# The block mask's room and place, two turns and six weight sums in another order (RWKV-6 attention, then a two-layer SiLU block)

## Chip, cores and metric

One core of one Trainium2 chip. The metric is device time in microseconds, from the launch to the end of the slowest (here the only) core. Before the change: 570.13 us, median of 3 runs (570.03 to 570.25). Engines are named as in the profile: PE (matrix products), PEld (its weight loads), DVE (VectorE), ACT (ScalarE), POOL (GpSimd), SP (the engine that issues most DMAs).

## The reference

Inputs r, k, v, w are (4 batches, 8 heads, 768 tokens, 48) in float32. First the recurrence of RWKV-6, then a bridge, then a two-layer block with SiLU:

```python
for t in range(S):
    cur = einsum('bhd,bhe->bhde', u[None] * k[:, :, t], v[:, :, t])
    y[:, :, t] = einsum('bhd,bhde->bhe', r[:, :, t], state + cur)
    state = w[:, :, t, :, None] * state + einsum('bhd,bhe->bhde', k[:, :, t], v[:, :, t])
x = y.transpose(0, 2, 1, 3).reshape(3072, 384)
h = x @ w_in                       # 384 x 2048
out = (h / (1 + exp(-h))) @ w_out  # 2048 x 384
```

## The kernel before

**Units.** The 768 tokens are cut into 6 chunks of 128, and the 4 batches into 2 pairs: 12 units, numbered 0 to 11 ("the fourth unit" is number 3). A unit goes through the attention of its chunk, and its 256 rows of x then go through the two layers. The attention is made level by level: at level l (0 to 6) blocks of 2^l tokens are joined, keys (tile tk) and queries (tile tr) are multiplied by products of w (tiles tw), PE forms scores, and a mask says which scores are kept (keep_masked, L715). The diagonal, the "bonus" with u, is added apart: own_mask (L334) in units 0 to 3, and from unit 4 on a bonus by blocks of 8 tokens, which needs another mask, the block mask (make_block_mask, L480; read by block_write, L565).

**Masks.** There is one int8 mask of 128 x 2 x 64 for each level 1 to 6 (L332). Those of levels 5 and 6 are read for units 0 and 1 alone; later units copy those scores with ACT (keep_level, L792, its L800). The block mask has a room of its own in the tile spare (L464), and is made in unit 3, in the group of mix that also holds prepare of level 5 (L995): one iota on POOL (L484), then two small operations and two masks on DVE (L486, L487, L489).

**Turns.** From unit 2 on, a unit's w, k and r are turned by DVE (turn, L347; its L361 is a transpose of 128 x 512, two for each name). After a turn of w POOL forms the products (product, L404; L410), after one of k ACT and POOL make the keys (odd_ones, L656; start_keys, L666; grow_own, L651; grow_keys, L642). Unit 3's turns stand in the first three groups of mix(3) (L987, L988).

**Update of the state.** update (L901) lets PE form the new part, ACT scales the old state (L927), and DVE adds the two (L932).

**Weights.** w_in and w_out come in 16 pieces. Each is rounded into a pair of parts by ACT (L228, L230, L236) and DVE (L247, L248) and put together by POOL (add_weight, L256; L260). Pieces 0 to 7 are w_in, 8 to 15 w_out. Two rooms of temps are shared by all pieces in turn, so ACT's L230 for a piece waits until POOL has added the piece two before it.

**The layers.** Units 0 to 2 have a plain first layer (up, L1073; L1078), unit 0 a plain second one (down, L1262; L1267). From unit 1 on the second layer is made by seven products in place of eight (quarter, L1304; L1329), for which DVE forms sums of gt (sums, L1287; L1300: four each time) and four sums of w_out (weight_sums, L1283; L1285, numbered 0 to 3 by "which"). From unit 3 on the first layer is also made of fewer products, twenty (first_part, L1194; L1185) in the order of ORDER (L1189). For these, sums of w_in are needed: weight_plan (L1099) names them, in_weight_sum (L1120; L1124) makes them on POOL or DVE. Name, operands and room of those that the change moves:

```python
"m": (e["m"], a[1, 2], a[2, 2], sub)
"q14": (e["q14"], a[1, 2], a[3, 2], add)
"u1": (a[2, 2], a[4, 1], a[3, 1], sub), "u": (a[2, 2], e["m1"], a[2, 2], add),
"q19": (a[2, 3], a[2, 3], a[2, 2], sub)
```

u and q19 are the left sides of products 11 and 19 of the first layer.

**What sets the order.** Nothing is scheduled: each engine runs its instructions in the order of the program, and waits for the others through semaphores. The order is written out by hand: lists of steps in do(...) for units 0 to 2 (L1378 to L1434), and for units 3 to 11 the groups that mix(i) returns (L961), with the steps of the layers put between the groups by their counts (L1436 to L1451). The steps of sums are added to groups at L1440 to L1446. The last list ahead of unit 3 is:

```python
do((sums, 1, 3), (y_state, 2), *both(y_values, 2), *both(update, 2), (move_x, 2), *blocks[5:])
```

A tile of a pool with bufs=1 that is taken again waits for the readers of the one before; ruk (L431) is such a tile, first taken in unit 3.

Of the kernel before, what the change touches and what calls it, by code (L numbers as in the profile page):

```python
# [8 lines left out]
F32 = mybir.dt.float32  # L9
BF16 = mybir.dt.bfloat16  # L10
I8 = mybir.dt.int8
# [27 lines left out]
def kernel(  # L39
# [11 lines left out]
    nc = tc.nc  # L51

    B, H, S, D = r.shape
    DM, DF = moe_w_in.shape
    L = 128
    NL = 7
    NB = 2
# [13 lines left out]
    BLK = 1 << FIRST  # L71


    const = ctx.enter_context(tc.tile_pool(name="const", bufs=1))
    pin = ctx.enter_context(tc.tile_pool(name="pin", bufs=1))
    pt = ctx.enter_context(tc.tile_pool(name="pt", bufs=2))
# [112 lines left out]
    spare = const.tile([128, NSPARE * 2 * TU], F32, name="spare")  # L189
# [132 lines left out]

    masks = {}
    first = {}
    for l in range(NL):
        c, ni = 1 << l, L >> (l + 1)

        first[l] = score[:, 0, 0].rearrange("p q t -> p (q t)")[:, l * 64:(l + 1) * 64].rearrange("p (i c) -> p i c", c=c)
        nc.gpsimd.iota(first[l], pattern=[[2 * c, ni], [0, c]], base=0, channel_multiplier=0,
                       allow_small_or_imprecise_dtypes=True)  # L330
        if l > 0:
            masks[l] = const.tile([128, NB, ni, c], I8, name=f"mask{l}")  # L332
    nc.gpsimd.memset(spread, 0.0)
    own_mask = const.tile([128, NB, L // 2, 2], I8, name="own_mask")  # L334
    for b in range(NB):
# [81 lines left out]
    ruk = {}  # L417
# [40 lines left out]
    room_b = spare[:, 0:768]  # L458
    at = 768
# [1 line left out]
    nc.gpsimd.memset(block_sums, 0.0)  # L461
    block_both = spare[:, at:at + NB * H * BLK].rearrange("p (b h s) -> p b h s", b=NB, h=H)
    at += NB * H * BLK
    block_mask = spare[:, at:at + NB * L // 4].bitcast(I8).rearrange("p (b i s) -> p b i s", b=NB, s=BLK)  # L464
    at += NB * L // 4
    assert at <= NSPARE * 2 * TU

    def at_rk(start, *dims):
# [10 lines left out]

    def make_block_mask():  # L480

        ids = spare[:, 0:2 * NB].rearrange("p (x b) -> p x b", x=2)
        index = room_b[:, 2 * NB:2 * NB + L].rearrange("p (i s) -> p i s", s=BLK)
        nc.gpsimd.iota(index, pattern=[[BLK, L // BLK], [0, BLK]], base=0, channel_multiplier=0,  # L484
                       allow_small_or_imprecise_dtypes=True)
        nc.vector.tensor_single_scalar(out=ids[:, 0].bitcast(I32), in_=tok_all, scalar=-BLK, op=ALU.bitwise_and)  # L486
        nc.vector.tensor_copy(out=ids[:, 1], in_=ids[:, 0].bitcast(I32))  # L487
        for b in range(NB):
            nc.vector.tensor_single_scalar(out=block_mask[:, b], in_=index, scalar=ids[:, 1, b:b + 1], op=ALU.is_equal)  # L489
# [465 lines left out]
    def both(fn, i, *args):  # L955
        return [(fn, i, b, *args) for b in range(NB)]
# [4 lines left out]
    def mix(i):  # L961
# [3 lines left out]
        def at(now, *steps):  # L965
            return steps if now else ()
# [17 lines left out]
               [*at(i < len(units) - NB, (turn_apart, i), (turn_k, i)), (y_state, i), *both(y_values, i), *at(ahead, *turns(i + 1)), *at(ahead and i > NFAST, *sum_steps(i + 1, 0, 1)),  # L984
                *at(i <= NFAST, (sums, i - 1, FH // 2 - 2)), *both(update, i), *at(not ahead, (move_x, i))]]
        if i < NPAIR:
            groups = [[*both(turn, i, "w"), (product, i, 0)],  # L987
                      [*both(turn, i, "k"), (odd_ones, i)], [*both(turn, i, "r"), (start_levels, i), (prepare_keys, i, 1)],  # L988
                      [(prepare, i, 1), *[(product, i, l) for l in range(1, NL)]],
                      [(burst, i, 1), (keep_level, i, 1)],  # L990
                      [(keep_level, i, 2), (go_on, i, 2)],
                      [(prepare, i, 3), (reverse_v, i), (bonus, i, 0), (bonus_sum, i, 0)],
                      [(bonus, i, 1), (burst, i, 3), (keep_level, i, 3), (bonus, i, 2)],
                      [(keep_level, i, 4), (go_on, i, 4), (bonus_sum, i, 1), (load_rk, i + 1), (load_u,)],
                      [(prepare, i, 5), (make_block_mask,)],  # L995
                      [(burst, i, 5), (keep_level, i, 5, 0), (keep_level, i, 6, 0), (go_on, i, 6), *at(i == NPAIR - 1, *both(turn, i + 1, "w")), (bonus_spread, i), (bonus_write, i, (0,)), (keep_level, i, 5, 1), (keep_level, i, 6, 1), (bonus_write, i, (1,))], *end]
            groups = list(zip(groups, (1, 1, 0, 2, 1, 1, 1, 1, 1, 2, 2, 1, 1)))
        else:
# [172 lines left out]
    def keep_banks():  # L1171

        for x in range(2):
            kept[f"h{x}"] = ps.tile([128, 512], F32, name="p_h", bufs=2)
            kept[f"o{x}"] = second[0].tile([128, 512], F32, name="p_o", bufs=2)
# [169 lines left out]
    def ups(i):  # L1345

        if i >= NFAST:
            made = [[(first_part, i, n)] for n in ORDER]
            if i == len(units) - 1:
                made[10].append((sums_of_x, i, 7))  # L1350
            made[17].append((sums, i, 0))
            made[-1].append((sums, i, 1, range(4) if i > NFAST else (0, 2)))
            return made
        steps = [[(up, i, m)] for m in range(FC // 2)]
        for m in range(FH // 2 - (1 if i == len(units) - 1 else 2)):

            steps[FH // 2 + 1 + m].append((sums, i, m))
        steps[-1].append((sums, i, FH // 2 - 1))
        return steps

    def downs(i):
        return [[(quarter, i, x)] for x in range(7)]

    def do(*steps):
        for fn, *args in steps:
            fn(*args)
# [39 lines left out]
    for m in range(1, 4):  # L1406
# [1 line left out]
    do((head_weight, 8), (join_weight, 7), (scores, 1, 5), (grow_keys, 1, 6), (add_weight,), (tail_weight, 8), (up, 0, 6),  # L1408
       (bonus_write, 1))

    do((scores, 1, NL - 1), (bonus, 2, 0), (bonus, 2, 1), (join_weight, 8), (add_weight,), (bonus_sum, 2, 0), (bonus, 2, 2), (in_weight_sum, nc.gpsimd, "m", "q14"), (up, 0, 7), (turn_apart, 1), *both(x_products, 1),
       (turn_k, 1), *both(x_copy, 1), (tail_weight, 9), (head_weight, 9),
       (join_weight, 9), (add_weight,), (in_weight_sum, nc.gpsimd, "q3", "q"), *both(update, 1), (up, 1, 0), (tail_weight, 10), (head_weight, 10), (bonus_sum, 2, 1), *both(turn, 2, "w"))
    blocks = block_loads(3)
# [6 lines left out]
    for m in range(6):  # L1421
# [5 lines left out]
    do(*blocks[0:2], (level, 2, 2), (prepare, 2, 3), (down, 0, 1, 0), (down, 0, 0, 3), (down, 0, 1, 1), (sums, 1, 0), (weight_sums, 0))  # L1427
    do(blocks[2], (burst, 2, 3), (keep_level, 2, 3), (keep_level, 2, 4), (go_on, 2, 4), (prepare, 2, 5), (reverse_v, 2), (down, 0, 1, 2),
       (bonus_spread, 2), (sums, 1, 1), *blocks[3:5], (down, 0, 1, 3))
    do((burst, 2, 5), (keep_level, 2, 5), (keep_level, 2, 6), (go_on, 2, 6), (bonus_write, 2), (up, 1, 6), (weight_sums, 1),  # L1430
       (load_values, 3), (turn_apart, 2), (turn_k, 2), (up, 1, 7), (weight_sums, 2), (sums, 1, 2))
    do((sums, 1, 3), (y_state, 2), *both(y_values, 2), *both(update, 2),
       (move_x, 2),
       *blocks[5:])  # L1434

    for i in range(3, len(units)):  # L1436
        steps = downs(i - 2) + ups(i - 1)
        groups = mix(i)
        if i == NTOK + 1:
            groups[4][0].append((weight_sums, 3))  # L1440
            for place, engine, names in ((7, nc.vector, ("n",)), (8, nc.vector, ("m1", "m2",)), (9, nc.vector, ("q12a", "q12",)), (9, nc.gpsimd, ("n13", "t",)), (11, nc.gpsimd, ("u1", "u", "q19",)),):
                groups[place][0].append((in_weight_sum, engine, *names))
        if i == NFAST + 1:
            keep_banks()
            for place, engine, names in ((5, nc.gpsimd, ("q7",)), (8, nc.gpsimd, ("q8", "q1",)), (9, nc.gpsimd, ("q5", "q9",)), (14, nc.gpsimd, ("q6", "q17",)),):
                groups[place][0].append((in_weight_sum, engine, *names))  # L1446
        for group, count in groups:
            do(*group)
            for step in steps[:count]:
                do(*step)  # L1450
            steps = steps[count:]  # L1451
# [34 lines left out]
```

## Time and profile before

| | |
|---|---|
| median of 3 timed runs | 570.13 us |
| the profiled execution | 571.49 us |
| its span, first to last instruction | 569.7 us |
| PE, PEld busy | 555.2, 516.5 us |
| DVE, ACT, POOL busy | 476.4, 274.6, 394.5 us |
| granted PE clock | 1.0 |
| PE's waits from 60 to 260 us / later | 4.6 us / none shown |

The span leaves 1.79 us of the profiled execution outside it. Busy time of an engine that is waiting for another does not count, so the share of PE (97%) says how little time PE has in which it does nothing. The unit of 42 us that repeats from 240 us on is PE's work alone. Unit 2 ends, by PE's matmuls of y, at 122 us, unit 3 at 167, unit 4 at 215.

In the views, a group of instructions is told as start, duration, engine, line, operation, output and inputs, count, and in brackets the idle time of that engine just before it and what ended it. The chain that ended last shows start, duration and what.

### The profile page before, as it was taken

The page shows a single profiled execution, that of the slowest core. Times are in us where ns is not written, and L with a number is a line of the kernel's source. Part 1 is how long each engine was busy: PE and PEld are TensorE (multiplying, and loading weights), DVE is VectorE, ACT ScalarE, POOL GpSimd, SP SyncE. Part 2 cuts the span into 40 slices and gives each one's busy share as a digit, 9 for nine tenths or more (in the row PEclk, how much of TensorE's full clock was granted, in tenths as well). Part 3 has the DMA queues.
Part 4 walks back from the last instruction along what each step waited for, and adds up shares of the span by engine and source line. Part 5 has one row for each costly group of instructions (what it writes and reads, how often), then busy time and mean ns, then how long its engine had stood idle before and what let it go on. Part 6 is the DMA issues. An engine that isn't in the chain of part 4 may idle for free.

```text
span 569.7 us, 18886 instructions
## 1 busy us (share of the span) xinstructions
PE 555.2 (97%) x7782; PEld 516.5 (91%) x7782; DVE 476.4 (84%) x744; ACT 274.6 (48%) x620; POOL 394.5 (69%) x447
## 2 busy tenths in 40 slices
PE   8989999999998999999999999999999999999997
PEld 7767776699888999899999999999999999999997
DVE  7979787988999889899989989989989989882250
ACT  5679686262371364274274274274274272371330
POOL 6998698709896998887796696696696696700000
PEclk9999999999999999999999999999999999999999
DMA  9856976445345355274465465465465462102000
GB/s 221 275 104 191 238 220 131 49 68 118 89 78 100 70 109 96 56 134 90 80 128 94 84 116 94 90 111 92 94 104 95 90 110 65 38 5 56 29 9 21
DMA packets 206485, 57.59 MB, mean 101 GB/s; under 512 B 186048, under 2 KB 198208, under 8 KB 206400
## 3 DMA queue, kind: packets, MB, share of 16 engines
q1 hardware_dynamic: 203712, 54.23, 46.2%
q10 hardware_dynamic: 2688, 2.16, 1.5%
q8 instruction: 61, 1.00, 0.8%
q14 instruction: 24, 0.20, 0.1%
HBM read 47.14 MB, written 9.18 MB: 99 GB/s over the span
## 4 chain that ended last, share of the span: by engine, by line
PE 70%; DVE 11%; POOL 8%; DMA 3%; ACT 3%; SPq 2%; issue 2%; DVEq 0%; POOLq 0%; ACTq 0%
PE p_o L1329 24%; PE p_o L1185 14%; PE p_h L1185 9%; PE p_h L1329 4%; PE p_m L1267 3%; PE p_h L1078 2%; PE p_sc L700 2%; PE p_m L864 2%; POOL tk L642 2%; DVE temps L1300 2%; PE p_sc L1329 2%; DVE score L718 2%; DMA raw<-in_k_dram 2%; PE p_m L843 1%; PE p_m L700 1%
## 5 line engine op out<-in xcount | busy, mean ns | idle before, releaser
L642 POOL TENSOR_TENSOR tk<-tk,tw 128x256 f32<-128x256 f32 x112 | 90.7, 830 | 7.5 <-DVE tw L410 3.2
L1329 PE MATMUL p_o<-own,temps 128*128 128x192 f32 x496 | 82.9, 326 | 1.6 <-DVE temps L1300 1.6
L1329 PEld LDWEIGHTS p_o<-own,temps 128*128 128x128 f32 x496 | 80.8, 190 | 2.0 <-DVE temps L1300 1.9
L1185 PE MATMUL p_o<-xt,w_in_sb 128*64 128x128 f32 x1152 | 72.3, 273 | 0.3 <-POOL w_in_sb L1124 0.3
L410 POOL TENSOR_TENSOR tw<-tw 128x256 f32<-128x256 f32 (+6 forms) x71 | 40.0, 563 | 44.8 <-DVE tw L361 41.3
L1078 PE MATMUL p_h<-xt,w_in_sb 128*128 128x256 f32 x288 | 66.1, 384 | 1.7 <-POOL w_in_sb L260 1.5
L1185 PEld LDWEIGHTS p_o<-xt,w_in_sb 128*64 128x64 f32 x1152 | 64.7, 137 | 0.7 <-POOL w_in_sb L1124 0.6
L1078 PEld LDWEIGHTS p_h<-xt,w_in_sb 128*128 128x128 f32 x288 | 53.6, 190 | 10.0 <-POOL w_in_sb L260 2.4
L493 POOL TENSOR_TENSOR ruk<-tokens_rk 128x384 f32<-128x384 f32 x48 | 53.7, 1138 | 3.9 <-DVE block_sums L530 2.0
L1329 PE MATMUL p_o<-w_out_sb,gt 128*128 128x192 f32 x308 | 54.5, 330 | 1.2 <-DVE ob L1337 1.2
L1329 PEld LDWEIGHTS p_o<-w_out_sb,gt 128*128 128x128 f32 x308 | 50.0, 190 | 2.2 <-DVE ob L1337 1.5
L624 DVE TENSOR_TENSOR tr<-tr,tw 128x512 f32<-128x512 f32 x57 | 49.7, 873 | 0.6
L651 POOL TENSOR_TENSOR tk<-tk,tw 128x256 f32<-128x256 f32 x32 | 24.8, 804 | 30.7 <-DVE tk L361 30.7
L1300 DVE TENSOR_TENSOR temps<-gt 128x512 f32<-128x512 f32 (+1 forms) x48 | 45.9, 992 | 0.0
L1334 ACT COPY partial<-p_o 128x192 f32<-128x192 f32 x31 | 9.8, 320 | 68.0 <-PE p_o L1329 61.2
L1209 ACT ACTIVATE gt<-p_o 128x512 f32<-128x512 f32 x45 | 26.0, 601 | 25.5 <-PE p_o L1185 25.4
L612 ACT COPY tk<-tk 128x256 f32<-128x256 f32 x52 | 20.9, 402 | 35.5 <-POOL tk L642 27.1
L718 DVE COPY_PREDICATED score<-mask,p_sc 128x512 f32<-128x512 int8 x42 | 31.2, 799 | 2.1 <-PE p_sc L700 1.9
L1329 PE MATMUL p_o<-w_out_sb,temps 128*128 128x192 f32 x176 | 30.4, 326 | 0.0
L1329 PE MATMUL p_h<-w_out_sb,gt 128*128 128x192 f32 x168 | 29.1, 326 | 0.0
L493 POOL TENSOR_TENSOR spare<-tokens_rk 128x384 f32<-128x384 f32 x24 | 28.5, 1199 | 0.6
L1329 PEld LDWEIGHTS p_o<-w_out_sb,temps 128*128 128x128 f32 x176 | 28.9, 190 | 0.0
(248 smaller groups left out, 1310.5 us busy)
## 6 DMA issues: line engine op xcount, KB each, us to landing
w_out_sb<-in_moe_w_in_dram SPq DMA_DIRECT2D x6, 768.0 KB, 7.8
turned<-yt SPq DMA_DIRECT2D x18, 192.0 KB, 2.7
xt<-turned SPq DMA_DIRECT2D x9, 384.0 KB, 3.3
w_out_sb<-in_moe_w_out_dram SPq DMA_DIRECT2D x4, 768.0 KB, 5.4
own<-in_moe_w_out_dram SPq DMA_DIRECT2D x4, 768.0 KB, 5.8
tokens_w<-in_w_dram SPq DMA_DIRECT2D x8, 384.0 KB, 4.4
tokens_rk<-in_r_dram SPq DMA_DIRECT2D x7, 384.0 KB, 4.4
tokens_rk<-in_k_dram SPq DMA_DIRECT2D x7, 384.0 KB, 5.5
```

Of the source, the lines that this page charges most:

```text
L410: engine.tensor_tensor(out=up, in0=t[:, :, 0::2], in1=t[:, :, 1::2], op=ALU.mult)
L493: mul = lambda out, one, two: nc.gpsimd.tensor_tensor(out=out, in0=one, in1=two, op=ALU.mult)
L612: nc.scalar.copy(out=keys(i, X[(l + 1) % 2] * L + c, [4 * c, blocks], [c, 2], [1, c]), in_=keys(i, NP * L + c, [4 * c, blocks], [NP * L + ...
L624: nc.vector.tensor_tensor(out=odd, in0=odd, in1=tw[i][l][:, :, 0::2][:, :, :, None].to_broadcast([128, Q, L >> (l + 1), c]), op=ALU.mult)
L642: nc.gpsimd.tensor_tensor(out=out, in0=have, in1=odd_products(i, l, b, *blocks), op=ALU.mult)
L651: nc.gpsimd.tensor_tensor(out=have, in0=have, in1=odd_products(i, l, b, [2, NP * ni]), op=ALU.mult)
L718: nc.vector.copy_predicated(out=dst, mask=masks[l][:, :, None].to_broadcast([128, NB, NP, ni, c]), data=sc[e].rearrange("p (b q) (i c) -> ...
L1078: nc.tensor.matmul(p_h[:, a, :], lhsT=w_in_sb[:, c, f * 128:(f + 1) * 128], rhs=xt[i][:, c, :], start=(a == 0 and c == 0), stop=(a == 1 an ...
L1185: nc.tensor.matmul(p[h:h + PD, q, :], lhsT=left[:, f:f + PD], rhs=right, start=first and q == 0, stop=q == 3, skip_group_check=True)
L1209: nc.scalar.activation(out=g(f, t), in_=have, func=AF.Silu)
L1300: nc.vector.tensor_tensor(out=out, in0=one, in1=two, op=op)
L1329: nc.tensor.matmul(p, lhsT=left(f), rhs=right[:, f, :], start=which in (0, 1, 3) and f == 0, stop=f == FH - 1, skip_group_check=True)
```

## The change

Five edits:

1. **The block mask's room.** The masks of levels 5 and 6 become halves of one tile, late_masks, and the block mask lies over both of them, not in spare any more. The small tables for making it lie in a tile ruk, not in spare.
2. **The block mask's place.** make_block_mask moves from unit 3 to unit 2, after go_on of level 6 and ahead of bonus_write.
3. **Unit 3's turns of w and k** move from the first groups of mix(3) to the last list of unit 2, behind sums(1, 3). In DVE's order they then stand ahead of the addition L932.
4. **Sum 3 of w_out** (weight_sums) stands behind burst and ahead of keep_level of its group; it stood behind both.
5. **Sums of w_in.** m and q14 (POOL) come right after the scores of level 6 of unit 1, ahead of unit 2's bonus; u1, u and q19 (POOL) move from group 11 of unit 3 to group 0 of unit 4. In POOL's order they stood ahead of unit 4's first product and L651; now behind them.

The order of instructions on PE, ACT and SP is the same before and after. The core of the diff:

```diff
+    late_masks = const.tile([128, 2, NB, L // 2], I8, name="late_masks")
...
-            masks[l] = const.tile([128, NB, ni, c], I8, name=f"mask{l}")
+            if l < NL - 2:
+                masks[l] = const.tile([128, NB, ni, c], I8, name=f"mask{l}")
+            else:
+                masks[l] = late_masks[:, l - NL + 2].rearrange("p b (i c) -> p b i c", c=c)
...
-    block_mask = spare[:, at:at + NB * L // 4].bitcast(I8).rearrange("p (b i s) -> p b i s", b=NB, s=BLK)
-    at += NB * L // 4
+    block_mask = late_masks[:].rearrange("p x b t -> p (x b t)").rearrange("p (b i s) -> p b i s", b=NB, s=BLK)
...
-        ids = spare[:, 0:2 * NB].rearrange("p (x b) -> p x b", x=2)
-        index = room_b[:, 2 * NB:2 * NB + L].rearrange("p (i s) -> p i s", s=BLK)
+        free = pt.tile([128, H, 2, D], F32, name="ruk", bufs=1).rearrange("p h s d -> p (h s d)")
+        ids = free[:, 0:2 * NB].rearrange("p (x b) -> p x b", x=2)
+        index = free[:, 2 * NB:2 * NB + L].rearrange("p (i s) -> p i s", s=BLK)
...
-            groups = [[*both(turn, i, "w"), (product, i, 0)],
-                      [*both(turn, i, "k"), (odd_ones, i)], [*both(turn, i, "r"), (start_levels, i), (prepare_keys, i, 1)],
+            groups = [[(product, i, 0)],
+                      [(odd_ones, i)], [*both(turn, i, "r"), (start_levels, i), (prepare_keys, i, 1)],
...
-                      [(prepare, i, 5), (make_block_mask,)],
+                      [(prepare, i, 5)],
...
-    do((scores, 1, NL - 1), (bonus, 2, 0), (bonus, 2, 1), (join_weight, 8), (add_weight,), (bonus_sum, 2, 0), (bonus, 2, 2), (in_weight_sum, nc.gpsimd, "m", "q14"), (up, 0, 7), (turn_apart, 1), *both(x_products, 1),
+    do((scores, 1, NL - 1), (in_weight_sum, nc.gpsimd, "m", "q14"), (bonus, 2, 0), (bonus, 2, 1), (join_weight, 8), (add_weight,), (bonus_sum, 2, 0), (bonus, 2, 2), (up, 0, 7), (turn_apart, 1), *both(x_products, 1),
...
-    do((burst, 2, 5), (keep_level, 2, 5), (keep_level, 2, 6), (go_on, 2, 6), (bonus_write, 2), (up, 1, 6), (weight_sums, 1),
+    do((burst, 2, 5), (keep_level, 2, 5), (keep_level, 2, 6), (go_on, 2, 6), (make_block_mask,), (bonus_write, 2), (up, 1, 6), (weight_sums, 1),
...
-    do((sums, 1, 3), (y_state, 2), *both(y_values, 2), *both(update, 2),
+    do((sums, 1, 3), *both(turn, 3, "w"), *both(turn, 3, "k"), (y_state, 2), *both(y_values, 2), *both(update, 2),
...
-            groups[4][0].append((weight_sums, 3))
-            for place, engine, names in ((7, nc.vector, ("n",)), (8, nc.vector, ("m1", "m2",)), (9, nc.vector, ("q12a", "q12",)), (9, nc.gpsimd, ("n13", "t",)), (11, nc.gpsimd, ("u1", "u", "q19",)),):
+            groups[4][0].insert(1, (weight_sums, 3))
+            for place, engine, names in ((7, nc.vector, ("n",)), (8, nc.vector, ("m1", "m2")), (9, nc.vector, ("q12a", "q12")),
+                                         (9, nc.gpsimd, ("n13", "t"))):
...
-            for place, engine, names in ((5, nc.gpsimd, ("q7",)), (8, nc.gpsimd, ("q8", "q1",)), (9, nc.gpsimd, ("q5", "q9",)), (14, nc.gpsimd, ("q6", "q17",)),):
+            for place, engine, names in ((0, nc.gpsimd, ("u1", "u", "q19")), (5, nc.gpsimd, ("q7",)), (8, nc.gpsimd, ("q8", "q1")),
+                                         (9, nc.gpsimd, ("q5", "q9")), (14, nc.gpsimd, ("q6", "q17"))):
```

## The prediction

> **What bounds the kernel.** I read the page's busy line first, then the waits of the engine it names, then the chain that ended last and the timelines of the other engines at the places where that engine waits.
>
> ```profile
> PE 555.2 (97%) x7782; PEld 516.5 (91%) x7782; DVE 476.4 (84%) x744; ACT 274.6 (48%) x620; POOL 394.5 (69%) x447
> ```
>
> PE is busy 555.2 of 569.7 us, so 14.5 us are not PE work. PE's waits in the window 60 to 260 us, where all the moved steps lie (columns: line, waited for, total us, times, longest):
>
> ```profile
> PE p_o L1329 <- DVE temps L1300: 1.6, 1, 1.6
> PE p_o L1329 <- DVE ob L1337: 1.2, 1, 1.2
> PE p_m L1267 <- POOL w_out_sb L260: 0.9, 1, 0.9
> PE p_m L700 <- POOL tk L642: 0.6, 2, 0.4
> PE p_o L1185 <- POOL w_in_sb L1124: 0.3, 1, 0.3
> ```
>
> After 260 us the same view is empty: PE never waits. So a microsecond won before 260 us is kept to the end, and no more can be won than these 4.6 us and a few gaps of 0.15. In time they stand at 85.99 (0.92), 134.59 (0.36), 179.62 (1.60), 202.99 (0.34), 232.67 (1.17) and 250.09 (0.22). PE's, ACT's and SP's instruction orders are the same in the changed program; only DVE's and POOL's differ. All steps are therefore priced by what they do to those waits.
>
> **Two sums sooner (m, q14).** Three lines of POOL's timeline (start, us, the rest; idle time in brackets):
>
> ```profile
> 67.59 0.99 POOL L436 TENSOR_TENSOR spare<-tokens_rk 128x384 f32<-128x384 f32 x1 [4.51 <-DMA tokens_rk<-in_k_dram]
> ...
> 73.87 1.29 POOL L1124 TENSOR_TENSOR in_sum<-w_in_sb 128x512 f32<-128x512 f32 x1
> 75.11 1.29 POOL L1124 TENSOR_TENSOR raw<-w_in_sb 128x512 f32<-128x512 f32 x1
> ```
>
> The two ops, 2.5 us, move into 4.5 us in which POOL only waits for tokens. Everything behind them that is ready moves up by up to 2.5: the addition of weight piece 9 (L260) from 76.34 to 73.9, piece 10 from 80.61 to 78.4, and piece 11 from 84.11 to about 82.0, where DVE's L248 for it (81.03 to 82) is last. Piece 11 is what PE waits for at 85.99, and it then ends at 83.8, before PE asks at 85.07: **0.92 goes**. The 0.15 before L700 at 87.70 waits for POOL's L666, also sooner: 0.15 goes. What is late next is ACT:
>
> ```profile
> 92.32 0.94 ACT L230 ACTIVATE temps<-temps,shift 128x768 uint32<-128x768 uint16 x1 [3.30 <-POOL w_out_sb L260]
> ```
>
> ACT itself waits for L260, so pieces 12 to 15 follow by 1.5 to 2.4 us. The tightest is piece 15: now its addition ends at 101.0 and the L1267 that reads it starts about then; after, 99.4 against 99.85. Cover if it fails: PE gives the 1.07 back there. Both ends: 0 and 1.07; I take 1.07, since ACT's wait of 3.30 us for POOL shows slack in the chain.
>
> **Block mask in unit 2 (L480).** DVE's four ops took 151.79 to 154.92, 3.1 us, because each stood behind a POOL op. The nearest undisturbed rows are L340 (128x64 int8 from f32, median 244 ns) and L314 (128x2 int32, median 375 ns): two masks, two small ops and gaps make an estimated 1 us; the ends are 0.8 and 3.1. The new place is before L598 at 115.90, where DVE waits 0.79 for ACT's L800 and POOL is idle from 111.2 to 128.5 (17.3 us), so the low row is the nearer one. Two tenths or so stick out; L850 on PE reads that score at 120.39 and L598 ended at 118.41, so 2 us cover them. At 3.1 the cover is short by about 0.3: PE would lose 0.3. The iota (0.30) goes into POOL's idle time; the new room (tile ruk) has no older reader, and its next writer is at 141.47.
>
> The 3.1 us that leave unit 3 do **not** reach PE by themselves. DVE would come 3.1 sooner to L591, but that waits for ACT's L590, which ended at 158.50 and hangs on PE's L700 at 154.87:
>
> ```profile
> 157.37 1.19 DVE tw L361 x2
> 158.56 0.17 DVE both_b L591
> 158.75 3.69 DVE score L598 x2
> 162.44 3.43 DVE temps L1300 x3
> ```
>
> Value: 0.
>
> **Unit 3's turns of w and k sooner, w_out sum 3 sooner.** DVE waits 1.37 us at 126.02 for ACT's L927; the four transposes (2.6 us; the data were issued by SP up to 106.4) now stand in that gap, less some 0.4 of issue. POOL's product then starts 1.9 sooner than 128.54, L666 and ACT's L612 follow, and L642 ends near 132.9 instead of 134.54: **the 0.36 at 134.59 goes** (PE asks at 134.23). Behind the turns wait L932 (its state is read by PE some 85 us later), L1337 and the turn of r, which still comes 0.5 sooner. The sum of 1.80 at 136.54 fills the 1.20 that DVE waits for PE at 134.28; its reader, the seventh quarter, is at 140.5. Ends: 0 and 0.36.
>
> **Three sums later (u1, u, q19).**
>
> ```profile
> 165.53 1.46 POOL L1124 TENSOR_TENSOR w_in_sb<-w_in_sb 128x512 f32<-128x512 f32 x1
> 167.06 1.33 POOL L1124 TENSOR_TENSOR w_in_sb<-raw,w_in_sb 128x512 f32<-128x512 f32 x1
> 168.48 1.34 POOL L1124 TENSOR_TENSOR w_in_sb<-w_in_sb 128x512 f32<-128x512 f32 x1
> ...
> 172.93 1.83 POOL L651 TENSOR_TENSOR tk<-tk,tw 128x256 f32<-128x256 f32 x2 [1.93 <-DVE tk L361]
> ```
>
> They take 4.25 us and go behind L651. Beside them DVE forms sums of gt (L1300):
>
> ```profile
> 112.83 0.42 DVE L1300 TENSOR_TENSOR temps<-gt 128x256 f32<-128x256 f32 x1
> ...
> 165.89 1.38 DVE L1300 TENSOR_TENSOR temps<-gt,temps 128x256 f32<-128x256 f32 x1
> 167.19 2.91 DVE L1300 TENSOR_TENSOR temps<-gt 128x256 f32<-128x256 f32 x2
> ```
>
> The same op is 0.42 with POOL idle and 1.3 to 1.45 beside it; the one at 165.89 ends at 167.27, 0.28 behind POOL's op (166.99). DVE gets one such op for each POOL op. So in old times: the first four L1300 still stand beside POOL's bonus work (to about 166.8), the next four run free, 4 x 0.44 = 1.7, and the turn of k starts at 168.8 instead of 172.14 (**3.3 sooner**). Then POOL runs two L651 (0.9 each), the three sums and the products. Four L1300 behind five POOL ops end near 174.6 instead of 176.3, L932 near 176.1, and the third L1300 of the last sum, which PE waits for, near 178.0 instead of 179.56. PE asks at 178.02. Of the 1.60 I leave 0.2: **1.4 go**, ends 0 and 1.6. The chain of waits names a DMA ahead of that turn; DVE's idle time there is only 0.40, and L651's 1.93 is really a wait for DVE.
>
> The Trainium skill, page "SBUF — State Buffer", section "Who interferes with whom", has VectorE and GpSimd sharing one port pair under an exclusive lock. It agrees with the 0.28 above and speaks against the move: without a lock the delayed sums would cost DVE nothing, all 1.6 would go, and the sum would be 567.1.
>
> POOL itself: L651 and the sums end near 175.7, 1.0 later than 174.72 with nothing deferred; it then has 2.02 idle before L493 at 180.96 and 0.95 before L642 at 183.87, both on work that now comes sooner. So 202.99 (0.34) and 232.67 (1.17, a chain that starts from PE at 195.8 and goes through two DMAs) stay as they are.
>
> **Sum.** 1.07 + 0 + 0.36 + 1.4 = 2.8 us. The profiled execution took 571.49 us, 1.79 outside its span; it becomes 568.7, its span 566.9. The median of the three timed runs is 1.36 below it; the same difference gives 570.13 - 2.8 = **567.3**.
>
> **Rivals.**
> - The stall at 179.62 stays, since the sums only block other L1300: saved 1.43, 568.7. For it: nine DVE ops still stand behind POOL. Against it: the turn of k comes sooner. 0.17.
> - Weight pieces are held by ACT or by their loads, and PE waits for piece 15 instead: saved 1.76, 568.4. For it: the margin of 0.45. Against it: ACT's 3.30 wait. 0.07.
> - Both, so that the change does little of what it moves things for: saved 0.36, 569.8. 0.08.
> - **Slower: POOL late for the first layer of unit 3.** If the turn of k keeps its time of 172.14, the three sums push POOL back 4.25; the idle 2.97 takes some up, and 1.28 arrives at q9, the sum that PE already waits for at 202.99. All that PE won before is lost there, and the time is 570.13 + 1.3 = 571.4. It decides once POOL's L642 of 183.87 starts later than now. For it: POOL is full from 184 to 205. Against it: four L1300 have no POOL op beside them. 0.10.
> - More: 202.99 and some of 232.67 go as well, up to 1.5 beyond the forecast: 565.8 to 566.6. 0.08.
>
> The forecast, 566.7 to 568.0, has 0.50. About 0.2% (1.14 us) is what a measurement of this kernel can tell from no change. Faster by more: 0.50 + 0.08 + 0.07 + three quarters of 0.17 = 0.78; within: 0.12; slower: 0.10. The range 566.2 to 570.2 leaves out the slower case and a part of the best.
>
> **What would show it.** Right: no PE wait for L260 near 85, none for L642 near 133, the block mask's ops about 0.3 us long near 114, L1300 at 0.42 just ahead of the turn of k, and under 0.4 of PE wait for L1300 near 176. Wrong: a wait for L260 near 99; a PE wait for score at L850; PE waits for L1124 near 200 of over a microsecond; or L1300 all at 1.3 up to the turn of k.

## The result and the profile after

The changed kernel takes **568.25 us** (median of 10 runs, 567.98 to 569.04) against 570.25 (10 runs, 569.46 to 572.69) for the kernel before on the same chip: a ratio of 0.9964 with a 95% interval from 0.9953 to 0.9975. That is 2.0 us less, and 1.4 to 2.7 by the interval. A second comparison, on another chip, gave 568.66 against 570.01: 0.9973, from 0.9963 to 0.9982. The forecast was 2.8 us less, 567.3; the range of 566.2 to 570.2 holds the time, the narrower forecast of 566.7 to 568.0 does not.

The profiled execution after took 568.89 us with a span of 567.1, at a granted clock of 1.0 as before. Its busy line, the answer to the first line of the prediction:

```profile
PE 555.3 (98%) x7782; PEld 517.6 (91%) x7782; DVE 477.7 (84%) x744; ACT 275.1 (49%) x620; POOL 395.4 (70%) x447
```

PE's busy time is the same; only what lies between has become less. In the changed kernel the numbers of lines are four higher than before from the masks on (L1300 is now L1304, L700 is L704, L1329 is L1333). PE's waits from 60 to 260 us (line, waited for, total us, times, longest):

```profile
PE p_o L1333 <- DVE ob L1341: 1.3, 1, 1.3
PE p_o L1189 <- POOL w_in_sb L1128: 0.8, 1, 0.8
PE p_m L704 <- POOL tk L646: 0.2, 1, 0.2
PE p_h L1082 <- POOL w_in_sb L260: 0.2, 1, 0.2
```

Three of the prediction's five lines are shorter or gone: L260 ahead of L1271 (0.9), the one for L646 at 134 (0.4) and L1304 (1.6). Two have grown: the sum q9 (L1128) from 0.34 to 0.83, and L1341 from 1.17 to 1.35. After 260 us PE still waits for nothing.

The same steps of PE in the two timelines tell where the time went:

| step of PE | before | after | difference |
|---|---|---|---|
| L1082, weight piece at the start | 63.13 | 63.89 | +0.76 |
| L704 behind the wait for piece 11 | 87.70 | 87.13 | -0.57 |
| a step behind piece 15 | 102.44 | 101.60 | -0.84 |
| L1333 behind L704's second group | 135.22 | 133.80 | -1.42 |
| sixth quarter of unit 2 (L1333) | 185.57 | 182.42 | -3.15 |
| L1189 that waits for q9 | 202.99 | 200.39 | -2.60 |
| L704 of unit 5 | 250.09 | 247.50 | -2.59 |
| span | 569.7 | 567.1 | -2.6 |

The largest step, 1.73 us, lies between 135 and 185, where the three sums were moved; half a microsecond is given back at q9.

### The profile page after: what moved, and what is told of

It is laid out like the page before. It is cut to its first block, busy times and chain, and to the rows that moved or that the text cites. A ratio compares the mean times of both kernels' runs of the same rounds, so it can differ in the third digit from the quotient of the medians.

```text
span 567.1 us, 18885 instructions
## 1 busy us (share of the span) xinstructions
PE 555.3 (98%) x7782; PEld 517.6 (91%) x7782; DVE 477.7 (84%) x744; ACT 275.1 (49%) x620; POOL 395.4 (70%) x447
## 4 chain that ended last, share of the span: by engine, by line
PE 73%; POOL 10%; DVE 6%; SPq 5%; DMA 3%; issue 2%; ACT 0%; ACTq 0%; DVEq 0%; POOLq 0%
PE p_o L1333 23%; PE p_o L1189 14%; PE p_h L1189 9%; PE p_h L1082 7%; PE p_h L1333 4%; PE p_m L1271 4%; SPq L127 3%; PE p_sc L704 2%; PE p_m L868 2%; POOL tk L646 2%; DMA raw<-in_w_dram 2%; PE p_sc L1333 2%; PE p_m L847 1%; PE p_m L704 1%; DMA w_out_sb<-in_moe_w_in_dram 1%
## 5 line engine op out<-in xcount | busy, mean ns | idle before, releaser
L646 POOL TENSOR_TENSOR tk<-tk,tw 128x256 f32<-128x256 f32 x112 | 93.0, 851 | 7.9 <-DVE tw L414 3.8
L1333 PE MATMUL p_o<-own,temps 128*128 128x192 f32 x496 | 82.8, 326 | 0.0
L1333 PEld LDWEIGHTS p_o<-own,temps 128*128 128x128 f32 x496 | 80.8, 190 | 0.2 <-DVE temps L1304 0.2
L1189 PE MATMUL p_o<-xt,w_in_sb 128*64 128x128 f32 x1152 | 72.2, 273 | 0.8 <-POOL w_in_sb L1128 0.8
L414 POOL TENSOR_TENSOR tw<-tw 128x256 f32<-128x256 f32 (+6 forms) x71 | 40.5, 571 | 41.4 <-DVE tw L365 38.0
L1082 PE MATMUL p_h<-xt,w_in_sb 128*128 128x256 f32 x288 | 66.1, 384 | 1.8 <-POOL w_in_sb L260 1.6
L1189 PEld LDWEIGHTS p_o<-xt,w_in_sb 128*64 128x64 f32 x1152 | 64.6, 137 | 1.1 <-POOL w_in_sb L1128 1.1
L1082 PEld LDWEIGHTS p_h<-xt,w_in_sb 128*128 128x128 f32 x288 | 53.6, 190 | 10.0 <-POOL w_in_sb L260 2.4
L1333 PE MATMUL p_o<-w_out_sb,gt 128*128 128x192 f32 x308 | 54.5, 330 | 1.3 <-DVE ob L1341 1.3
L497 POOL TENSOR_TENSOR ruk<-tokens_rk 128x384 f32<-128x384 f32 x48 | 53.1, 1127 | 2.5 <-DMA tokens_rk<-in_k_dram 2.5
L628 DVE TENSOR_TENSOR tr<-tr,tw 128x512 f32<-128x512 f32 x57 | 51.9, 910 | 1.0 <-PE p_m L704 0.4
L1333 PEld LDWEIGHTS p_o<-w_out_sb,gt 128*128 128x128 f32 x308 | 50.0, 190 | 2.4 <-DVE ob L1341 1.6
L655 POOL TENSOR_TENSOR tk<-tk,tw 128x256 f32<-128x256 f32 x32 | 24.7, 800 | 31.6 <-DVE tk L365 31.6
L1304 DVE TENSOR_TENSOR temps<-gt 128x512 f32<-128x512 f32 (+1 forms) x48 | 43.1, 934 | 0.0
L1333 PE MATMUL p_o<-w_out_sb,temps 128*128 128x192 f32 x176 | 30.4, 326 | 0.0
L722 DVE COPY_PREDICATED score<-mask,p_sc 128x512 f32<-128x512 int8 x38 | 28.4, 806 | 1.4 <-PE p_sc L704 1.3
L1333 PE MATMUL p_h<-w_out_sb,gt 128*128 128x192 f32 x168 | 29.1, 326 | 0.0
L497 POOL TENSOR_TENSOR spare<-tokens_rk 128x384 f32<-128x384 f32 x24 | 28.5, 1200 | 0.6
L1333 PEld LDWEIGHTS p_o<-w_out_sb,temps 128*128 128x128 f32 x176 | 28.9, 190 | 0.0
```

What stands on the lines that cost most here:

```text
L414: engine.tensor_tensor(out=up, in0=t[:, :, 0::2], in1=t[:, :, 1::2], op=ALU.mult)
L497: mul = lambda out, one, two: nc.gpsimd.tensor_tensor(out=out, in0=one, in1=two, op=ALU.mult)
L628: nc.vector.tensor_tensor(out=odd, in0=odd, in1=tw[i][l][:, :, 0::2][:, :, :, None].to_broadcast([128, Q, L >> (l + 1), c]), op=ALU.mult)
L646: nc.gpsimd.tensor_tensor(out=out, in0=have, in1=odd_products(i, l, b, *blocks), op=ALU.mult)
L655: nc.gpsimd.tensor_tensor(out=have, in0=have, in1=odd_products(i, l, b, [2, NP * ni]), op=ALU.mult)
L722: nc.vector.copy_predicated(out=dst, mask=masks[l][:, :, None].to_broadcast([128, NB, NP, ni, c]), data=sc[e].rearrange("p (b q) (i c) -> ...
```

## Experiments

Each kernel is the one before or the one after with the edit shown; its times stand beside runs of the kernel before on the same chip.

### The three sums alone

```diff
 (before)
-  ..., (11, nc.gpsimd, ("u1", "u", "q19",)),):
+  ...,):
...
-  in ((5, nc.gpsimd, ("q7",)), ...
+  in ((0, nc.gpsimd, ("u1", "u", "q19")), (5, nc.gpsimd, ("q7",)), ...
```

> Before, with only u1, u and q19 deferred to unit 4; the block mask is still made in unit 3. The account: the four L1300 ahead of unit 4's turn of k run at 0.42 us, the turn comes about 3 us sooner, PE's wait of 1.6 for L1300 near 179 falls to 0.2 or less, and up to 0.5 is given back at q9 near 203: 0.9 to 1.5 less than before. Rival (it is the removal of the mask's 3.1 us from DVE that does it, and deferring POOL's sums only loads unit 4): the wait near 179 stays and the one for q9 near 203 grows by 1.3: about 1.3 more than before.

Measured: 568.65 (11 runs) against 570.35, ratio 0.9973 (0.9964 to 0.9982): **1.7 us, 1.0 to 2.1**. The wait for L1300 near 179 is gone, and the one for q9 grew by 0.2, to 0.56. The gain is a little above the 0.9 to 1.5 that was expected, within its interval. This is most of the whole change.

### The changed kernel with the three sums put back

```diff
 (after)
-  in ((0, nc.gpsimd, ("u1", "u", "q19")), (5, ...
+  in ((5, ...
...
+  ... (9, nc.gpsimd, ("n13", "t")), (11, nc.gpsimd, ("u1", "u", "q19"))):
```

> The changed kernel with only u1, u and q19 put back into unit 3. If the deferral is the main term (alone it took 1.7 us off), PE's wait for L1300 near 178 is back at 1.4 to 1.7 and the time is 0.6 to 1.0 below before, 1.0 to 1.4 above the changed kernel. Rival (the parts are interchangeable, each filling the same DVE time): within 0.4 of the changed kernel.

Measured: median 569.67 (11 runs, one at 572.65) against 570.23, ratio 1.0 (0.9987 to 1.0012). The median is 1.4 above that of the changed kernel, as expected for the main term; that it would still be 0.6 to 1.0 below the kernel before is not shown. Two of PE's waits in this kernel are

```profile
PE p_o L1333 <- DVE temps L1304: 1.9, 1, 1.9
...
PE p_o L1189 <- POOL w_in_sb L1128: 0.3, 1, 0.3
```

The stall returns, larger than before the change since PE comes sooner, and the wait for q9 is 0.3 again. So the two belong together: what the three sums win at 176, they cost in part at 200.

### The two sums alone

```diff
 (before)
-do((scores, 1, NL - 1), (bonus, 2, 0), ..., (bonus, 2, 2), (in_weight_sum, nc.gpsimd, "m", "q14"), (up, 0, 7), ...
+do((scores, 1, NL - 1), (in_weight_sum, nc.gpsimd, "m", "q14"), (bonus, 2, 0), ..., (bonus, 2, 2), (up, 0, 7), ...
```

> Before, with only m and q14 moved ahead of unit 2's bonus. The account of the prediction: PE's wait of 0.92 us for piece 11 (L260, near 86 us) and the 0.15 ahead of L700 go, and nothing after that takes them back: 1.1 us less than before, up to 1.4 if the piece 15 products also stop running late; PE's wait of 1.6 for L1300 near 179 stays. Rival (the weight chain is held by ACT or by loads): 0 to 0.3 less, with a PE wait for L260 somewhere between 85 and 101.

Measured: 570.03 (11 runs) against 570.35, ratio 0.9996 (0.9987 to 1.0005): **no gain clear of noise**, 0.3 by the medians and at most 0.7. The edit does what it says. POOL's timeline in this kernel (idle time in brackets):

```profile
63.42 1.27 POOL L1124 TENSOR_TENSOR in_sum<-w_in_sb 128x512 f32<-128x512 f32 x1
64.65 1.27 POOL L1124 TENSOR_TENSOR raw<-w_in_sb 128x512 f32<-128x512 f32 x1
66.94 1.02 POOL L436 TENSOR_TENSOR spare<-tokens_rk 128x384 f32<-128x384 f32 x1 [1.01 <-DMA tokens_rk<-in_k_dram]
...
78.88 1.83 POOL L260 TENSOR_TENSOR w_out_sb<-temps 128x768 uint32<-128x768 uint32 x1 [0.96 <-ACT temps L228]
...
82.36 1.83 POOL L260 TENSOR_TENSOR w_out_sb<-temps 128x768 uint32<-128x768 uint32 x1
```

The sums fill the wait for tokens; part of what POOL wins it then spends waiting for ACT's part of a weight piece (0.96), and PE has no wait near 85, nor for L260 anywhere up to 101, as the rival had it. But three kernels that leave this stretch alone (the three sums, the mask, the turns) have little or none for piece 11 either. In the execution with the three sums alone, POOL and then PE:

```profile
65.83 1.02 POOL L436 TENSOR_TENSOR spare<-tokens_rk 128x384 f32<-128x384 f32 x1 [2.78 <-DMA tokens_rk<-in_k_dram]
...
82.34 1.83 POOL L260 TENSOR_TENSOR w_out_sb<-temps 128x768 uint32<-128x768 uint32 x1
```

```profile
84.87 1.45 PE L1267 MATMUL p_m<-w_out_sb,gt 128*128 128x384 f32 x4
```

The tokens landed at 65.8 instead of 67.6, piece 11 was ready at 84.17, and PE did not wait for it (it waited 0.41 just behind, at 86.74, for DVE's L624). From the start of L436 to the end of that L260 it is 18.3 us in all four executions with the old order (67.59, 66.67, 65.83, 65.83 to 85.94, 85.01, 84.17, 84.18), and PE's wait was 0.92, 0.19, 0 and 0. So the wait of 0.92 belonged to one execution, in which the tokens were late.

That is not yet what the move is worth, since a loss can also show at other steps. PE's way from its step L819 near 66 us to L909 of unit 2 near 121 (L823 and L913 where the lines have moved) contains all of them. In the eight profiled executions that have the two sums sooner (late tokens, below, left aside) it is 54.60 to 54.65 us, whether POOL's L436 started at 65.70 or at 67.45. In the four with the old order it is 56.20 (before), 55.49 (the mask alone), 55.00 (the three sums alone) and 54.65 (the turns). So the move takes away a loss that differs from one execution to the next: 1.6, 0.9, 0.4 and 0.

### Late tokens, with and without the two sums

To show that the wait follows the tokens, the loads of unit 2's tokens were issued later, in the kernel before and in the one with the two sums moved.

```diff
 (before, and before with the two sums sooner)
-others = {1: [(bonus_sum, 1, 0), (bonus_sum, 1, 1), (load_rk, 2)], 2: [*both(update, 0), *blocks[8:10]],
+others = {1: [(bonus_sum, 1, 0), (bonus_sum, 1, 1)], 2: [*both(update, 0), *blocks[8:10], (load_rk, 2)],
```

> The kernel before with one edit: the loads of unit 2's tokens are issued behind another weight piece's load and eight loads of r (SP issued those from 61.2 to about 70), so the tokens land some 6 to 9 us later. Theory A: the PE's wait at 85.99 in the profiled execution of before (0.92 for piece 11 of L260) follows the landing of the tokens, because POOL stands behind them in order: from the start of L436 to the end of that L260 it took 18.3 us in every execution so far, and PE asks at about 84.9. Then with L436 at 73 to 76 the wait is 6.4 to 9.4 us and the kernel takes 576 to 580. Rival B: that wait has another cause (ACT's or DVE's part of the weight pieces): it stays below 1 us and the time stays at 570.2 to 571.

> The kernel before with the sums m and q14 sooner (as in the changed kernel) and the same late tokens. Theory A: two sums of 1.25 us are done while POOL waits, so the wait for piece 11 is 2.5 us shorter than in the kernel with late tokens alone, 4 to 7 us, and the time is 2.5 us less than that one's, 573.5 to 577.5: the edit is worth something only where the tokens are late. Rival B: no difference between the two, both at 570.2 to 571. Rival C, that the pieces wait for ACT's part (L228) here too: the difference is under 1 us.

Measured, beside 570.01 for the kernel before: 574.67 without the two sums sooner (5 runs, ratio 1.0081, 1.0067 to 1.0095) and 573.42 with them (5 runs, 1.0056, 1.0043 to 1.0068). POOL with late tokens, old order:

```profile
70.81 1.01 POOL L436 TENSOR_TENSOR spare<-tokens_rk 128x384 f32<-128x384 f32 x1 [7.25 <-DMA tokens_rk<-in_k_dram]
...
87.32 1.82 POOL L260 TENSOR_TENSOR w_out_sb<-temps 128x768 uint32<-128x768 uint32 x1
```

and with the two sums sooner:

```profile
72.26 1.01 POOL L436 TENSOR_TENSOR spare<-tokens_rk 128x384 f32<-128x384 f32 x1 [5.69 <-DMA tokens_rk<-in_k_dram]
...
86.46 1.82 POOL L260 TENSOR_TENSOR w_out_sb<-temps 128x768 uint32<-128x768 uint32 x1
```

The tokens came less late than expected, so the times are lower too, but the rule holds to the tenth: 70.81 + 18.3 = 89.1, and L260 ended at 89.14; with the two sums sooner it takes 16.0, 2.3 less. The medians are 1.25 us apart, half of the 2.5 that was expected, and single runs of the two overlap. In the two profiled executions, PE's way from L819 to L909 is 58.97 and 58.08, 0.9 less with the sums sooner although its tokens landed 1.45 later. PE's waits are not where theory A had them: in the old order 2.4 of its 3.3 from 80 to 92 are for L260; with the sums sooner none is, but 2.11 at L1078 for ACT's L1087, which stands behind ACT's wait for DVE's part of a weight piece, and 0.98 for DVE's L624. **Rival B falls, and theory A stands for POOL's part**; rival C, a difference under 1 us because the other engines' parts of the pieces are late, is not excluded: POOL's 2.3 speak against it, PE's waits in part for it. The two sums are worth something where the tokens are late, and from 0 to 0.9 in the three ordinary executions above.

### The mask alone, and the changed kernel with the mask made in unit 3

First edits 1 and 2 of the change alone (room and place):

```diff
 (before)
+    late_masks = const.tile([128, 2, NB, L // 2], I8, name="late_masks")
...
-                      [(prepare, i, 5), (make_block_mask,)],
+                      [(prepare, i, 5)],
...
+    do((burst, 2, 5), (keep_level, 2, 5), (keep_level, 2, 6), (go_on, 2, 6), (make_block_mask,), (bonus_write, 2), ...
```

> Before, with only the block mask's room and place changed (made in unit 2). The account: DVE comes about 3 us sooner to L591 and waits there for ACT's L590, so the time is the same within 0.3 us, PE's wait of 1.6 for L1300 near 179 stays, and PE does not wait at L850. Rival (the mask's 3.1 us stood on the way to that wait): 1.6 less than before and no wait near 179.

Then the changed kernel with the new room and the old place:

```diff
 (after)
-                      [(prepare, i, 5)],
+                      [(prepare, i, 5), (make_block_mask,)],
...
-    do((burst, 2, 5), (keep_level, 2, 5), (keep_level, 2, 6), (go_on, 2, 6), (make_block_mask,), (bonus_write, 2), ...
+    do((burst, 2, 5), (keep_level, 2, 5), (keep_level, 2, 6), (go_on, 2, 6), (bonus_write, 2), ...
```

> The changed kernel with the block mask made in unit 3 again, in its new room. If moving it is worth nothing because DVE then waits for ACT's L590 or has its other operations blocked behind POOL's instead: the time of the changed kernel within 0.3 us, and DVE's start of L602 near 157 to 159 is the same within 0.5. Rival (the mask's time in unit 3 does come off the chain once the deferred sums free POOL): 0.8 or more above the changed kernel, with a PE wait for L1304 near 176.

Measured: 570.11 (11 runs, ratio 0.9997, 0.9988 to 1.0005) and 568.28 (6 runs against 570.23, ratio 0.9982, 0.996 to 1.0003; its median is that of the changed kernel). The mask's place is worth nothing that these runs can tell (the second interval is wide), though its four ops became much shorter. In the kernel before they stood beside POOL's work:

```profile
151.79 1.23 DVE L486 TENSOR_SCALAR spare<-tok_all 128x2 int32<-128x2 int32 x1
...
153.33 1.67 DVE L489 TENSOR_SCALAR spare<-spare 128x128 int8<-128x128 f32 x2
```

and in the changed kernel POOL is idle beside them:

```profile
113.72 0.16 DVE L490 TENSOR_SCALAR ruk<-tok_all 128x2 int32<-128x2 int32 x1
...
114.19 0.48 DVE L493 TENSOR_SCALAR late_masks<-ruk 128x128 int8<-128x128 f32 x2
```

### The turns and the w_out sum

```diff
 (before: edits 3 and 4 of the change alone)
+do((sums, 1, 3), *both(turn, 3, "w"), *both(turn, 3, "k"), (y_state, 2), ...
...
+groups[4][0].insert(1, (weight_sums, 3))
```

> Before, with only unit 3's turns of w and k and w_out sum 3 moved. The account: PE's wait of 0.36 for L642 near 134 goes, nothing else: 0.3 to 0.6 less than before, and DVE's wait of 1.37 for L927 goes. Rival (DVE is the bound of unit 3, so what its idle time takes in there comes off the stall near 179 as well): 1.5 to 2 less.

Measured: 569.62 (11 runs) against 570.35, ratio 0.9988 (0.9979 to 0.9997): **0.7 us, 0.2 to 1.2**. PE's wait at 134 is gone; the one for L1300 remains with 1.7. PE's way from L909 of unit 2 to L909 of unit 3 is 45.07 to 45.11 us in every execution with the old place and 44.48 or 44.49 in every one with the new: 0.6.

### Where PE's remaining waits come from: q9, and unit 5's block sums

First, q5 and q9 move from group 9 of unit 4 to group 8, right behind q8 and q1:

```diff
 (after)
-(8, nc.gpsimd, ("q8", "q1")), (9, nc.gpsimd, ("q5", "q9")),
+(8, nc.gpsimd, ("q8", "q1", "q5", "q9")),
```

> The changed kernel with q5 and q9 on POOL ahead of go_on of level 4 in unit 4, not behind it. If the wait of 0.83 us for q9 near 200 is where part of the change's gain is given back: that wait goes, and the time is 0.6 to 0.9 below the changed kernel, 2.6 to 2.9 below before. Rival (the keys that POOL now makes 2.6 later take its place, a PE wait for L646 near 202, or the next wait for DVE near 230 takes it up): within 0.2 of the changed kernel.

Then, with that edit kept, unit 5's third group of block sums (the L534 with which DVE waits for POOL) moves from ahead of the fourth quarter to behind the fifth:

```diff
-keys_2 = [(odd_keys, i, 2), (grow_keys, i, 2, False), (grow_queries, i, 2), *sum_steps(i, 2)]
+keys_2 = [(odd_keys, i, 2), (grow_keys, i, 2, False), (grow_queries, i, 2), *at(i > NPAIR + 1, *sum_steps(i, 2))]
...
-([*at(i in (NPAIR + 1, len(units) - 1), (sums_of_x, j, 0, 1)), ...
+([*at(i == NPAIR + 1, *sum_steps(i, 2)), *at(i in (NPAIR + 1, len(units) - 1), (sums_of_x, j, 0, 1)), ...
```

> As the run before, and in unit 5 DVE forms the third group of block sums (L534) behind the fifth quarter, not ahead of it, so that the addition that PE waits for near 230 (1.35 us) does not stand behind DVE's wait for POOL. If both waits are separate: 1.9 to 2.2 below the changed kernel, about 4.1 below before. Rival (DVE's addition then waits for something else, or the steady stretch behind 240 is set by a loop that does not pass through that wait): no more than the run before.

Measured: 568.45 (7 runs, ratio 0.9972) and 568.39 (7 runs, ratio 0.9971), both as the changed kernel, where 0.6 to 0.9 and 1.9 to 2.2 less were expected. Waits were removed and the time stayed. PE's largest wait with q9 sooner, where L1128 is not in the list any more:

```profile
PE p_o L1333 <- DVE ob L1341: 1.5, 1, 1.5
```

and with unit 5's sums later as well:

```profile
PE p_o L1189 <- DVE temps L1341: 0.6, 1, 0.6
PE p_o L1189 <- DVE p_o L1216: 0.5, 1, 0.5
PE p_o L1333 <- DVE ob L1341: 0.3, 1, 0.3
```

The 0.8 for q9 is gone in the first, but a wait of 0.2 for DVE came in its place and the next one grew by 0.2; in the second the 1.5 became three waits of 1.3 in all (0.56, 0.51 and 0.25). PE comes to L913 of unit 4 at 211.03 and 211.32 instead of 212.04 (212.24 in the changed kernel's second profile), but to L704 of unit 5 at 246.99 and 247.39 instead of 247.50 (247.73): from L913 to L704 it takes 0.5 to 0.6 longer. That points to something other than PE as what sets the time there.

### What sets it: unit 5's turn of k

In the chain that ended last of the changed kernel, the stretch from 203 to 247 us holds no work of PE's. It goes through DVE's L573, L365 and L1304 to the turn of k of unit 5, over POOL up to 237, and over DVE and ACT to PE's L704 at 247.50. POOL's timeline of the changed kernel has the place:

```profile
215.18 1.49 POOL L414 TENSOR_TENSOR tw<-tw 128x512 f32<-128x512 f32 x1
218.64 1.65 POOL L655 TENSOR_TENSOR tk<-tk,tw 128x256 f32<-128x256 f32 x2 [1.97 <-DVE tk L365]
```

Six L1304 stood ahead of that turn on DVE; two of them are read by PE only some 5 us later. In the two kernels above POOL still waits 1.25 there, and L655 starts at 218.12 and 218.42. The experiment puts these two L1304 behind the turn:

```diff
 (after)
-made[17].append((sums, i, 0))
+made[17].append((sums, i, 0, range(4) if i > NFAST else (0, 2)))
...
-*at(j == NPAIR, (sums, j - 1, 1, (1, 3)))
+*at(j == NPAIR, (sums, j - 1, 0, (1, 3)), (sums, j - 1, 1, (1, 3)))
```

> The changed kernel with one edit: two of the four L1304 ahead of the fifth unit's turn of k (the two that are needed five us later) stand behind it. Theory: between 204 and 247 a chain over DVE and POOL sets the time, not PE; POOL stood 1.97 us at 216.7 for that turn. Then L655 starts at 216.7 to 217.2 instead of 218.64, the wait of 1.35 near 230 becomes 0 to 0.6, PE's L704 at 247.50 starts 0.8 to 1.9 sooner, and the kernel takes 0.8 to 1.9 less than the changed kernel: 566.4 to 567.5. Rival: PE's own work sets it and the waits are separate: only what the wait near 230 loses, or nothing where DVE at 221 to 226 is now the late one: 568.0 to 568.4.

> The changed kernel itself, beside the others on this chip: 568.25 as before, 568.0 to 568.6, 2.0 less than the kernel before. Its profiled execution shows again the wait of 0.8 for q9 at 200 and 1.3 near 230 if both belong to the kernel; if the first belongs to that one execution, 0.3 to 0.6.

Measured on one chip: **567.49** with the edit (5 runs, 566.89 to 567.68) and 568.66 for the changed kernel (9 runs, 568.08 to 569.13), beside 570.01 for the one before. The ratio to the kernel before is 0.9951 (0.9939 to 0.9964), and its runs do not overlap those of the changed kernel: 1.2 us less, the fastest of all. The changed kernel's second profile has 0.79 for q9 and 1.38 near 230 again, so both waits belong to the kernel. With the edit, POOL and two waits of PE:

```profile
214.57 1.49 POOL L414 TENSOR_TENSOR tw<-tw 128x512 f32<-128x512 f32 x1
216.02 1.65 POOL L655 TENSOR_TENSOR tk<-tk,tw 128x256 f32<-128x256 f32 x2
```

```profile
PE p_o L1189 <- POOL w_in_sb L1128: 0.8, 1, 0.8
PE p_o L1333 <- DVE ob L1341: 0.3, 1, 0.3
```

POOL no longer waits, and PE's wait near 230 is 0.31 instead of 1.38 (the changed kernel's second profile): 1.07 of the 1.17. This wait had shrunk as far in the kernel with unit 5's sums later (0.25), where L655 stood at 218.42 and nothing was won; now L655 starts at 216.02 and the time falls. **So the chain over DVE and POOL set the time there.** Of the 1.97 us closed, POOL keeps 1.05 at the end of its chain (L497 ends at 236.04 instead of 237.70, and 0.61 of that was there before the turn) since some of its next ops take longer (L414 1.99 instead of 1.47, L655 1.89 instead of 1.43). Whether the wait for q9 (0.8) is worth removing in this kernel was not tried.

## Why the prediction was right, and where it was not

- **Three sums later: right in mechanism, and in size.** Predicted 1.4 (ends 0 and 1.6), measured 1.7 alone (1.0 to 2.1). DVE's timeline of the changed kernel ahead of the turn of k:

```profile
164.90 1.15 DVE L1304 TENSOR_TENSOR temps<-gt,temps 128x256 f32<-128x256 f32 x1
165.97 0.74 DVE L1304 TENSOR_TENSOR temps<-gt 128x256 f32<-128x256 f32 x2
166.64 0.41 DVE L1304 TENSOR_TENSOR temps<-temps,gt 128x256 f32<-128x256 f32 x1
167.09 0.42 DVE L1304 TENSOR_TENSOR temps<-gt,temps 128x256 f32<-128x256 f32 x1
167.91 1.31 DVE L365 STREAM_TRANSPOSE tk<-raw 128x512 f32<-128x512 f32 x2 [0.40 <-DMA raw<-in_r_dram]
...
170.73 1.48 DVE L1304 TENSOR_TENSOR temps<-temps,gt 128x256 f32<-128x256 f32 x1
```

  The last beside POOL takes 1.15, the next four 0.37 to 0.42 each, and behind the turn, beside POOL again, 1.48: as reckoned. Counted from L591 (L595 after the change), the turn of k comes 3.3 us sooner with the three sums alone (157.33 to 167.66, against 158.54 to 172.14), the very figure forecast. The third L1304 of the last sum, the one that PE waits for, ends at 176.42, not near 178.0, because the work before it had also moved (L595 starts 1.42 sooner than L591 did). The margin is thin: in the second profile of the changed kernel PE waits 0.65 there, more than the 0.4 that was named as the limit.
- **The lock rule of the Trainium skill** (page "SBUF — State Buffer", section "Who interferes with whom") agrees with the trace: the delayed sums did cost DVE time beside them. The L1304 of 1.48 ended at 172.21, 0.28 behind POOL's op (171.93); beside no POOL op it takes 0.41. They were not free, but they cost where there was room.
- **Two sums sooner: the step that failed.** "0.92 goes" was true of the profiled execution, and is only in part a saving of the kernel. That execution took 571.49, 1.36 above the median of its runs, and the wait of 0.92 was part of this excess: it came with tokens that landed 0.9 to 1.8 us later than in the three others with the old order. I subtracted it all the same from the median, which contains it only in part: the loss that the move takes away was 1.6 in that execution and 0.9, 0.4 and 0 in those three. In place of 1.07 the timed runs show 0.3, and 0.7 at most. The mechanism holds (POOL's sums fill its wait, and no execution with them sooner has the loss); the size was that of one execution.
- **Turns and w_out sum: right, and a little too small.** 0.36 forecast, 0.7 measured with an interval from 0.2 to 1.2, and 0.6 by PE's steps; the wait at 134 went. Where the other 0.2 comes from was not followed up.
- **Mask: right, 0.** The reason given was half of what happened. From its first masking of the stretch (L718, at 143.96) to L591 DVE takes 14.58 us in the kernel before, and 14.57 from L722 to L595 with the mask alone moved. There it waits 1.02 at 155.32 for PE's L704 and then 0.44 for ACT's L594, the path that the prediction named; but half of the 3.1 never becomes free, since two L1128 that now stand beside POOL take 3.43 together instead of 1.85. In the changed kernel the stretch is 14.58 again.
- **"202.99 (0.34) and 232.67 (1.17) stay as they are": wrong by 0.7.** They became 0.83 and 1.35. POOL's work up to q9 is 2.6 us sooner, PE 3.15. This is the place that the slower rival named, but 0.5 is given back there, not all that was won and 1.3 more. And "a microsecond won before 260 us is kept to the end" holds only where PE is what comes last: removing q9's wait gave nothing that could be measured, since the chain over DVE and POOL ended near the same 247.
- **The sum.** The parts measured alone are 1.7, 0.7, 0.3 and 0.2 (mask), 2.9 in all; the whole is 2.0 and 1.35 in two comparisons. Each part is uncertain by half a microsecond, so whether anything but the 0.7 above is lost between them stays open. That the range held is owed in part to its width: it reaches to 570.2, no change at all. 568.25 lies next to the 568.4 of the rival in which PE waits for piece 15 instead, and that is chance: PE waits for no weight piece after 64 us in the changed kernel.

## What to carry to other kernels

A wait in one profiled execution is a saving only if the timed runs contain it: where that execution is slower than the median, look at which of its waits hang on a DMA's landing, and take their size from several executions, over a stretch long enough to hold every place where the loss can show. Where PE's waits are removed and the time stays, follow the chain that ended last over the engines between two such waits: the gap to close was POOL's 1.97 us for a transpose, which gave 1.2, not PE's 0.8, which gave nothing. On DVE, what is read late should stand behind what another engine waits for.

## What was not expected of the hardware

- The same loads landed at different times: POOL's L436, which starts when unit 2's tokens are there, stood at 65.83, 65.83, 66.67 and 67.59 in four executions of kernels with the same order up to there. PE's wait for the weight piece behind it was 0, 0, 0.19 and 0.92.
- The smallest DVE ops suffer most beside POOL: 128x2 int32 took 1.23 us beside it and 0.16 with POOL idle, 128x128 to int8 0.84 and 0.24 each (both shown above), as if each stood behind an op of POOL's. The 128x2 cast between them (L487) started at 153.05, as one POOL op had ended and 0.02 before the next began, and took 0.17.
